# A pre-LN attention and GLU block: row-sum reciprocals and scalings two steps later, filler products ahead of a head group's first V products, and Q rows asked for at the third key tile

## Chip, cores and metric

One core of a Trainium2 chip. The metric is the device time of one execution in microseconds; the time of the kernel before is the median of three runs. The engines are PE (TensorE, matrix products), PEld (its weight loads), DVE (VectorE), ACT (ScalarE), POOL (GpSimd) and SP (SyncE, which here issues nearly all DMAs, in the program's order).

## The reference

A block of 2048 tokens and model width 512, with 32 heads of 16, followed by a gated layer of width 1792. All inputs are bfloat16.

```python
def _A_ref(x, wqkv, wo):
    B, S, D = x.shape
    H = 32
    Dh = D // H
    qkv = (lambda x, *d: x.transpose(*d))((x @ wqkv).reshape(B, S, 3, H, Dh), 2, 0, 3, 1, 4)
    q, k, v = qkv[0], qkv[1], qkv[2]
    scores = jnp.einsum("bhqd,bhkd->bhqk", q, k) * (Dh ** -0.5)
    p = _softmax(scores, axis=-1)
    o = jnp.einsum("bhqk,bhkd->bhqd", p, v)
    return (lambda x, *d: x.transpose(*d))(o, 0, 2, 1, 3).reshape(B, S, D) @ wo

def _B_ref(x, w_gate, w_up, w_down):
    g = jnp.einsum("bsd,df->bsf", x, w_gate)
    u = jnp.einsum("bsd,df->bsf", x, w_up)
    h = _sigmoid(g) * u
    return jnp.einsum("bsf,fd->bsd", h, w_down)

x = A_x
h = x + _A_ref(_layernorm(x, axis=-1), A_wqkv, A_wo)
h2 = h + _B_ref(_layernorm(h, axis=-1), B_w_gate, B_w_up, B_w_down)
return h2
```

With 32 heads and 2048 x 2048 scores each, the kernel takes 134 million exponentials, and these are what most of its time goes to.

## The kernel before

**Stages.** A prologue normalizes x and makes K of the first eight heads, the first Q rows and some of V. Then one long loop runs over the queries in five chunks (three of 512 columns, two of 256) and in each chunk over eight head groups of four heads. One unit is one key tile of one head: 128 keys against 512 queries, or two such tiles against 256 queries. Three units make a step; there are 683 steps (NS), and a head group takes 21.3 of them in a 512 chunk and 10.7 in a 256 chunk.

**A step** (the loop at L963). `emit_scores` (L764) issues the scores of three units into one of two PSUM buffers `pss` (L783) and one exponential of ACT over the whole buffer into a slot `pt` (L794). Every fourth step is split: two units go to ACT, and the third goes to DVE, which makes its exponential in parts: bits (L813) in the same step, the first part (L816, L819) one step later, the second (L822) two and the third (L826) three steps later. In the steps of the set `twice`, in all chunks but the first and at most every twelfth step, a second step of the cycle is split too, with scratch in `OT`.

**V products.** The tiles of probabilities are multiplied with V a cycle of four steps later, by a plan made at the start (`plan_pv`, L925). `emit_pv` (L857) adds 4 products for each key tile to the one accumulator `acc` (L864). Where the first key tile of a new group falls in the middle of a cycle, its V products are planned one step later than the rest (L933), since `acc` must be copied out first.

**The end of a head group.** After its last V products `emit_norm` (L834) copies `acc` to `xs_all` on DVE (L838), and SP sends the four row sums to DRAM (L841) and brings them back spread over 128 partitions (L842). Five steps later `recip` takes the reciprocals on DVE (L849), writes them to DRAM (L851) and reads them back broadcast, in four DMAs, to `rb_all` (L853). Five steps after that `scale` multiplies `xs_all` by `rb_all` into `OT` (L845), which the output projection reads (L506). `later(i, fn)` (L872) puts a function into the list `due` of step i.

**Q rows.** The scores read Q from two buffers `QB`, by turns. The rows of the next group are fetched by `emit_q_rows` (L217, four DMAs, L223) and `emit_q_bound` (L226, two DMAs, L233). In a 512 chunk these are issued in the program at key tile 12 of 16 of the running group (L788), in a 256 chunk at its first. SP does not wait for the step: it issues each DMA as soon as those ahead of it in its queue are out and what the DMA itself depends on is done.

**Filler.** What else there is to do (V, K and Q of the other heads, then for each finished chunk the output projection, the layer norm and the gated layer) is written as a generator, `filler` (L742), that yields costs and waits. `emit_fill` (L879) takes some of it in each step, by rates that depend on the step's place in its cycle of four and on how many V products the step has (L755). These products all use one PSUM bank, `pm`, so a new block waits until DVE or ACT has read the one before (up_mul L543, tanh L535, the copies L157, L430 and L551).

**Order within a step.** All engines run in the program's order (`manual_schedule`). In each step come first the scores and ACT's exponential, then the V products due, then the functions in `due`, then the filler (L969 to L974):

```python
for u in pv_due.pop(i, []):
    emit_pv(*u[:3], i)
for fn in due.pop(i, []):
    fn()
if 1 <= i < NS:
    emit_fill(i)
```

After the loop `ffn_last` (L652) does the last chunk's projection and gated layer by itself.

Of the kernel before, what the change touches and what calls it, by code (L numbers as in the profile page):

```python
# [18 lines left out]
def kernel(  # L19
# [19 lines left out]
    NG = H // 4  # L39
# [4 lines left out]
    NC = len(CHUNKS)  # L44
    NQC = S // QC
    GU = 3
    CYC = 4
    RATES = ((2.0, 2.0, 0.0, 3.0), (2.0, 2.5, 0.0, 3.0))
    FIRST = 44
    GM = 188  # L50
    G1 = 680
    QS = DH ** -0.5 * 1.4426950408889634 * 2.0 ** 23
    LEAD = 0.106445681
# [161 lines left out]
    qgs = [(c, g) for c in range(NC) for g in range(NG)]  # L215

    def emit_q_rows(n):  # L217
        c, g = qgs[n]
        q0, w = CHUNKS[c]
        assert ("q", q0 // QC, g // 2) in ready  # L220
        for j in range(4):
            r = 64 * (g % 2) + DH * j
            nc.sync.dma_start(out=QB[n % 2][32 * j:32 * j + 32:2, j, 0:w],  # L223
                              in_=QTu[r:r + DH, g // 2, q0:q0 + w])
# [167 lines left out]
    def per_bank(c):  # L392
        return QC // CHUNKS[c][1]
# [6 lines left out]
    NS = len(groups)  # L400
# [363 lines left out]
    def emit_scores(i):  # L764
        group = groups[i]
        n = len(group)
        pss = pss2[(i + 1) % 2]
        idle = i >= 3 * FIRST and (state["done"] or state["wait"] > i + CYC)
        pairs = i < FIRST or (i % 2 == 1 or i - i % CYC + 2 in twice) and not idle
        order = list(enumerate(group))  # L770
        if pairs and group[0][3] // 2 == group[1][3] // 2:
            order[1:] = order[:0:-1]
        n_of = max(per_bank(u[0]) for u in group)
        parts = [(ui, u, h) for h in range(n_of) for ui, u in order[:2] if h < per_bank(u[0])]
        parts += [(ui, u, h) for ui, u in order[2:] for h in range(per_bank(u[0]))]
        for ui, (c, g, k, j), h in parts:
            n_qg = c * NG + g
            w = CHUNKS[c][1]
            kt = k * per_bank(c) + h
            assert ("k", g // 2) in ready  # L780
            h0 = 64 * (j // 2)
            rows = slice(h0, h0 + 64) if pairs else slice(0, P)
            nc.tensor.matmul(pss[:, ui, h * w:(h + 1) * w], lhsT=KT[rows, g, kt * P:(kt + 1) * P],  # L783
                             rhs=QB[n_qg % 2][rows, j, 0:w], start=True, stop=True,
                             tile_position=(h0, 0) if pairs else None)
        for c, g, k, j in group:
            n_qg = c * NG + g
            if k == (12 if per_bank(c) == 1 else 0) and j == 3 and n_qg + 1 < len(qgs):  # L788
                emit_q_rows(n_qg + 1)
                emit_q_bound(n_qg + 1)  # L790
        slot = i % 7
        pt = pt4[slot] if slot < 4 else (pt_early if i < GM else pt_late)[slot - 4]
        na = n - 1 if i in split else n
        ex = nc.scalar.activation(out=pt[:, 0:na, :], in_=pss[:, 0:na, :], func=ACT.Exp, scale=DH ** -0.5 / QS)  # L794
        if na < n:
            scratch = scratch_of(i)
            tc.declare_no_dep(exp_bits(pss[:, na, :], *scratch).ins, ex.ins,
                              reason="both only read, from different banks")
            later(i + 1, lambda: exp_first(*scratch))
            later(i + 2, lambda: exp_second(*scratch))  # L800
            later(i + 3, lambda: exp_third(pt[:, na, :], *scratch))
        for ui, u in enumerate(group):
            p_of[u] = pt[:, ui, :]

    def scratch_of(i):
        if i % CYC:
            flat = OT[(int((i - 20) / SPC) + 1) % 2][:].rearrange("p g q -> p (g q)")
            return (flat[:, 0:2 * QC].bitcast(mybir.dt.int32), flat[:, 2 * QC:4 * QC].bitcast(mybir.dt.int32),
                    flat[:, 4 * QC:6 * QC].bitcast(FP32))
        return early_scratch if i < GM else late_scratch  # L810

# [17 lines left out]
    def norm_part(t, w, n):  # L829
        k = t.shape[1] * w // QC  # L830
        o = k * (n % (QC // w))
        return t[:, o:o + k]

    def emit_norm(c, g, i):  # L834
        w = CHUNKS[c][1]
        b = w // 32
        xs, rb, s32, r32 = (norm_part(t, w, g) for t in (xs_all, rb_all, s32_all, r32_all))
        nc.vector.tensor_copy(out=xs, in_=acc[:, 0:w])  # L838
        sd = dram.tile([4, w], FP32, name="sd", tag="sd%d" % w)
        for j in range(4):  # L840
            nc.sync.dma_start(out=sd[j:j + 1, :], in_=xs[32 * j + DH:32 * j + DH + 1, :])  # L841
        nc.sync.dma_start(out=s32, in_=sd[:].rearrange("j (a b) -> (j a) b", b=b))  # L842

        def scale():
            nc.vector.tensor_tensor(out=OT[c % 2][:, g, 0:w], in0=xs, in1=rb, op=ALU.mult)  # L845
            ready.add(("o", c, g))

        def recip():
            nc.vector.reciprocal(out=r32, in_=s32)  # L849
            rd = dram.tile([4, w], FP32, name="rd", tag="rd%d" % w)  # L850
            nc.sync.dma_start(out=rd[:].rearrange("j (a b) -> (j a) b", b=b), in_=r32)  # L851
            for j in range(4):
                nc.sync.dma_start(out=rb[32 * j:32 * j + 32, :], in_=rd[j:j + 1, :].to_broadcast([32, w]))  # L853
            later(i + 10, scale)
        later(i + 5, recip)

    def emit_pv(c, g, k, i):  # L857
        w = CHUNKS[c][1]
# [13 lines left out]
    def later(i, fn):  # L872
        due.setdefault(i, []).append(fn)
# [5 lines left out]
    def emit_fill(i):  # L879
        state["step"] = i  # L880
        r = rate(i)
        if not r or state["done"] or i < state["wait"]:
            state["debt"] = 0.0
            return
        state["debt"] += state["rate"] or r
        while state["debt"] > 0 or isinstance(state["next"], tuple):
            c = state["next"]
            state["next"] = next(fl, None)
            if c is None:
                state["done"] = True  # L890
                return
            if isinstance(c, tuple):
                kind, n = c
                if kind == "rate":
                    state["rate"] = n
                    continue
                state["debt"] = 0.0
                state["wait"] = i + 1 + n if kind == "gap" else i + 1 + (n - i - 1) % CYC if kind == "at" else n
                return
            state["debt"] -= c  # L900
# [5 lines left out]
    def load_w():  # L906
# [4 lines left out]
        for f in (0, 7):  # L911
            later(GM + 21 + f // 2, lambda f=f: nc.sync.dma_start(out=wd[:, f:f + 7, :], in_=wd_v[:, f:f + 7, :]))

    LAG = 2

    split = set(range(8, G1, CYC))
    twice = set()
# [7 lines left out]
    def plan_pv():  # L925
        plan, last = {}, 0
        for n, group in enumerate(groups):
            if n < G1:
                if n % CYC == 0:
# [12 lines left out]
    with tc.manual_schedule():  # L942
        p1ctx = ExitStack()
        pmh["pool"] = p1ctx.enter_context(tc.tile_pool(name="ps_p1", bufs=6, space=PSUM))
        prologue(p1ctx.enter_context(tc.tile_pool(name="pro", bufs=1)))
        p1ctx.close()
        pmh["pool"] = ps_misc
        sctx = ExitStack()
        ps_s = sctx.enter_context(tc.tile_pool(name="ps_s", bufs=1, space=PSUM))
        ptp = sctx.enter_context(tc.tile_pool(name="ptp", bufs=1))  # L950
        pss2 = [ps_s.tile([P, GU, QC], FP32, name=f"pss{k}") for k in range(2)]
        pt4 = [ptp.tile([P, GU, QC], BF16, name=f"pt{k}") for k in range(4)]
        for g4 in (0, 4):
            later(60 + g4, lambda g4=g4: nc.gpsimd.memset(wo_pad[:, g4:g4 + 4, :], 0.0))
        later(72, load_wo)
        for n in range(4):
            r = slice(32 * n, 32 * n + 32)
            nc.gpsimd.tensor_copy(out=same[r], in_=ident_bf[r, r].unsqueeze(1).to_broadcast([32, 4, H]))
        later(90, lambda: nc.gpsimd.tensor_copy(out=ident_f[:], in_=ident_bf[:]))
        load_w()  # L960
        pv_due = plan_pv()
        n_pv = {i: len(us) if i < G1 + CYC else 0 for i, us in pv_due.items()}
        for i in range(NS + LAG):  # L963
            if i < NS:
                emit_scores(i)
            if i == NS + LAG - 1:
                while next(fl) == 1:
                    pass
            for u in pv_due.pop(i, []):  # L969
                emit_pv(*u[:3], i)  # L970
            for fn in due.pop(i, []):
                fn()
            if 1 <= i < NS:
                emit_fill(i)  # L974
        for _ in fl:
            pass
        sctx.close()
        pmh["pool"] = ctx.enter_context(tc.tile_pool(name="ps_t", bufs=6, space=PSUM))
        pmh["work"] = ctx.enter_context(tc.tile_pool(name="tail", bufs=4))
        assert not due  # L980
        ffn_last(NC - 1)
# [30 lines left out]
```

## Time and profile before

| what | value |
|---|---|
| median of 3 runs | 963.77 us (963.26 to 965.14) |
| the profiled execution, its own time | 962.96 us |
| span of its instructions | 961.1 us |
| granted TensorE clock, mean | 1.000 |
| ACT busy, 35 to 100 us | 60.3 of 65.0 us |
| ACT busy, 932 us to the end | 5.8 of 29.1 us |
| first and last exponential of the loop start | 34.24 and 929.73 us |
| DMA, mean share of 16 engines over the span | q1 10.4%, q10 0.5% |

The span runs from the first instruction to the last; the time of the same execution is 1.86 us longer. In a row of a group of instructions stand line, engine and operation, the tiles it writes and reads with their shapes, the count, the busy time, the mean length in nanoseconds, and the engine's idle time just before these instructions with what ended it. In the timeline a row has start, length, engine, line and tiles, and in brackets the idle time ahead of it. Starts of PE's products of 512 columns lie about 0.215 us apart when nothing holds them up, although each row lasts some 0.38 us; the rows overlap.

### The profile page before, as it was taken

How to read it: one execution, taken by the hardware profiler on the slowest of the kernel's cores; microseconds unless marked ns; L12 is line 12 of the kernel's file. 1: busy time of each engine (PE TensorE's matmuls, PEld its weight loads, DVE VectorE, ACT ScalarE, POOL GpSimd, SP SyncE). 2: the span in 40 equal slices, each digit the busy share in tenths (PEclk: the TensorE clock that was granted, in tenths of full speed). 3: DMA queues.
4: the chain of work that ended last, by engine and by line, in shares of the span. 5: the costliest groups of instructions: out<-in, count | busy, mean ns of one | idle time of the engine just before them, and what ended most of it. 6: DMA issues, size and time to landing. Idle time of an engine off the chain costs nothing.

```text
span 961.1 us, 17150 instructions
## 1 busy us (share of the span) xinstructions
PE 826.7 (86%) x6327; PEld 337.8 (35%) x6425; DVE 788.1 (82%) x1428; ACT 895.3 (93%) x767; POOL 41.5 (4%) x49
## 2 busy tenths in 40 slices
PE   4887888888788999988788999988788999888998
PEld 2322222222222332222222233222355555455646
DVE  8589998888788888899888888888888788777653
ACT  4789999999999999999999999999998999899872
POOL 4700000000000000000000000000000000000000
PEclk9999999999999999999999999999999999999999
DMA  5001350000013000000011000001011000110010
GB/s 160 21 8 50 114 117 17 16 16 2 16 26 103 16 16 17 19 12 26 14 27 26 16 16 15 14 15 26 16 31 23 16 13 13 27 32 16 9 35 12
DMA packets 37500, 28.38 MB, mean 30 GB/s; under 512 B 17708, under 2 KB 32776, under 8 KB 37416
## 3 DMA queue, kind: packets, MB, share of 16 engines
q1 hardware_dynamic: 35828, 25.71, 10.4%
q10 hardware_dynamic: 1588, 1.58, 0.5%
q8 instruction: 50, 0.82, 0.4%
q14 instruction: 34, 0.28, 0.1%
HBM read 20.31 MB, written 2.61 MB: 24 GB/s over the span
## 4 chain that ended last, share of the span: by engine, by line
PE 40%; DVE 26%; ACT 23%; issue 7%; DMA 3%; SPq 1%; ACTq 0%; DVEq 0%; POOL 0%; POOLq 0%
PE pss L783 20%; ACT pt L794 12%; PE acc L864 8%; PE pm L530 6%; ACT stg L794 4%; ACT wd L794 4%; DVE stg L813 3%; ACT QTu L794 2%; PE pm L546 2%; DVE reg L816 2%; DVE st L139 2%; DVE pt L826 2%; DVE y L822 2%; PE pm L506 2%; DVE reg L543 1%
## 5 line engine op out<-in xcount | busy, mean ns | idle before, releaser
L783 PE MATMUL pss<-QB,KT 64*128 64x512 bf16 (+3 forms) x2542 | 475.8, 336 | 86.9 <-ACT pt L794 43.8
L794 ACT ACTIVATE pt<-pss 128x1536 bf16<-128x1536 f32 (+1 forms) x392 | 501.1, 1363 | 16.3 <-PE pss L783 12.0
L783 PEld LDWEIGHTS <-KT 64*128 64x128 bf16 (+1 forms) x2560 | 181.4, 95 | 345.3 <-issue 232.5
L794 ACT ACTIVATE stg<-pss 128x1536 bf16<-128x1536 f32 (+1 forms) x140 | 183.1, 1355 | 4.6 <-PE pss L783 3.8
L813 DVE TENSOR_SCALAR stg<-pss 128x512 int32<-128x512 f32 x123 | 84.8, 689 | 69.3 <-PE pss L783 53.0
L864 PE MATMUL acc<-pt,Vaug 128*17 128x512 bf16 (+1 forms) x1471 | 112.5, 338 | 4.5 <-DVE xs_all L838 3.2
L794 ACT ACTIVATE wd<-pss 128x1536 bf16<-128x1536 f32 (+1 forms) x80 | 103.8, 1390 | 2.7 <-PE pss L783 2.4
L794 ACT ACTIVATE QTu<-pss 128x1024 bf16<-128x1024 f32 (+1 forms) x71 | 95.5, 1345 | 1.7 <-PE pss L783 1.2
L819 DVE SCALAR_TENSOR_TENSOR y<-reg 128x512 f32<-128x512 f32 x123 | 85.2, 692 | 4.2
L822 DVE SCALAR_TENSOR_TENSOR y<-y,reg 128x512 f32<-128x512 f32 x123 | 84.2, 684 | 1.1
L864 PEld LDWEIGHTS <-Vaug 128*17 128x17 bf16 x2560 | 50.4, 89 | 96.1 <-issue 80.8
L530 PE MATMUL pm<-reg,reg 128*128 128x512 bf16 (+1 forms) x252 | 55.6, 333 | 8.7 <-DVE reg L543 6.6
L530 PE MATMUL pm<-reg,wu 128*128 128x512 bf16 (+1 forms) x280 | 58.1, 338 | 1.5 <-ACT sg L535 1.2
L546 PE MATMUL pm<-wd,reg 128*128 128x512 bf16 x173 | 51.2, 381 | 5.7 <-issue 2.9
L146 POOL TENSOR_TENSOR rs<-ve,pw_neg 128x1 f32<-128x1 f32 (+1 forms) x24 | 17.7, 736 | 888.9 <-DVE ve L144 758.0
L816 DVE TENSOR_SCALAR reg<-stg 128x512 int32<-128x512 int32 x123 | 52.0, 423 | 2.0
L864 PE MATMUL acc<-stg,Vaug 128*17 128x256 bf16 (+1 forms) x564 | 50.6, 326 | 0.6 <-DVE stg L826 0.4
L543 DVE SCALAR_TENSOR_TENSOR reg<-sg,pm 128x512 bf16<-128x512 f32 x56 | 38.2, 682 | 13.9 <-PE pm L530 13.5
L826 DVE SCALAR_TENSOR_TENSOR pt<-y,stg 128x512 bf16<-128x512 f32 x70 | 47.8, 683 | 1.8
L535 ACT ACTIVATE sg<-pm 128x512 f32<-128x512 f32 x56 | 35.6, 637 | 10.1 <-PE pm L530 9.8
L813 DVE TENSOR_SCALAR wd<-pss 128x512 int32<-128x512 f32 x45 | 30.9, 688 | 15.9 <-PE pss L783 14.9
L165 PE MATMUL pm<-reg 128*128 128x512 bf16 x112 | 35.6, 391 | 2.2 <-issue 0.8
(129 smaller groups left out, 707.5 us busy)
## 6 DMA issues: line engine op xcount, KB each, us to landing
rb_all<-rd SPq DMA_DIRECT2D x96, 64.0 KB
reg<-in_A_x_dram SPq DMA_DIRECT2D x8, 256.0 KB
xr<-in_A_x_dram SPq DMA_DIRECT2D x16, 128.0 KB
out_dram<-ob SPq DMA_DIRECT2D x15, 128.0 KB
rb_all<-rd SPq DMA_DIRECT2D x60, 32.0 KB
KT<-stg SPq DMA_DIRECT2D x7, 256.0 KB
reg<-in_B_w_gate_dram SPq DMA_DIRECT2D x4, 448.0 KB
wu<-in_B_w_up_dram SPq DMA_DIRECT2D x4, 448.0 KB
```

What stands on the lines that cost most here:

```text
L165: nc.tensor.matmul(ps[:], lhsT=wqkv_sb[:, c, w0:w0 + P], rhs=xnT[:, c, n * QC:(n + 1) * QC], start=(c == 0), stop=(c == DC - 1))
L530: nc.tensor.matmul(ps[:, i * w:(i + 1) * w], lhsT=wt[:, c, f * P:(f + 1) * P], rhs=hnT[:, c, 0:w], start=(c == 0), stop=(c == DC - 1))
L543: nc.vector.scalar_tensor_tensor(out=out, in0=a, scalar=1.0, in1=b, op0=ALU.add, op1=ALU.mult)
L546: nc.tensor.matmul(ps[:], lhsT=hT[:, f, tt * P:(tt + 1) * P], rhs=wd[:, f, :], start=(f == 0), stop=(f == FC - 1))
L783: nc.tensor.matmul(pss[:, ui, h * w:(h + 1) * w], lhsT=KT[rows, g, kt * P:(kt + 1) * P], rhs=QB[n_qg % 2][rows, j, 0:w], start=True, stop= ...
L794: ex = nc.scalar.activation(out=pt[:, 0:na, :], in_=pss[:, 0:na, :], func=ACT.Exp, scale=DH ** -0.5 / QS)
L813: return nc.vector.tensor_scalar(out=e_bits, in0=src, scalar1=ONE_BITS, scalar2=0.0, op0=ALU.add, op1=ALU.max)
L816: nc.vector.tensor_scalar(out=e_man, in0=e_bits, scalar1=0x7FFFFF, scalar2=-0x40800000, op0=ALU.bitwise_and, op1=ALU.bitwise_or)
L819: nc.vector.scalar_tensor_tensor(out=e_pol, in0=m, scalar=PA, in1=m, op0=ALU.add, op1=ALU.mult)
L822: nc.vector.scalar_tensor_tensor(out=e_pol, in0=e_pol, scalar=PB, in1=e_man.bitcast(FP32), op0=ALU.add, op1=ALU.mult)
L826: nc.vector.scalar_tensor_tensor(out=dst, in0=e_pol, scalar=PC, in1=e_bits.bitcast(FP32), op0=ALU.add, op1=ALU.mult)
L864: nc.tensor.matmul(acc[32 * j:32 * j + VW, 0:w], lhsT=Vaug[:, kt, 4 * g + j, :], rhs=p[:, h * w:(h + 1) * w], start=(kt == 0), stop=(kt == ...
```

## The change

Three edits.

1. `emit_norm` takes the reciprocals seven instead of five steps after the group's last V products, and the scaling twelve instead of ten. The last group of each chunk, and of the last chunk the last two, keep five and ten. That is 34 of the 39 groups that go through `emit_norm`.
2. In a step (from step 8 on) whose planned V products contain the first key tile of a group, the filler of this step is issued ahead of those V products, and not at the step's end. The rate is the same; where a step has three sets of V products it is 0, so nothing moves there. In the order in which the built program's instructions stand, 22 blocks of filler move: one to four products at 512 columns, or eight at 256.
3. In the chunks of 512 columns, Q rows for the next group are asked for at the third key tile (k == 2) of the running group from group 6 on (`EARLY`; groups are counted through all chunks). The 256 chunks keep the first key tile, the first six groups the thirteenth (k == 12).

```diff
+    EARLY = range(6, 64)
...
         for c, g, k, j in group:
             n_qg = c * NG + g
-            if k == (12 if per_bank(c) == 1 else 0) and j == 3 and n_qg + 1 < len(qgs):
+            if k == (0 if per_bank(c) > 1 else 2 if n_qg in EARLY else 12) and j == 3 and n_qg + 1 < len(qgs):
                 emit_q_rows(n_qg + 1)
                 emit_q_bound(n_qg + 1)
...
     def emit_norm(c, g, i):
         w = CHUNKS[c][1]
         b = w // 32
+        wait = 2 if g < NG - 1 - (c == NC - 1) else 0
...
-            later(i + 10, scale)
-        later(i + 5, recip)
+            later(i + 10 + wait, scale)
+        later(i + 5 + wait, recip)
...
-            for u in pv_due.pop(i, []):
+            us = pv_due.pop(i, [])
+            early_fill = i >= 2 * CYC and any(u[2] == 0 for u in us)
+            for u in us:
+                if early_fill and u[2] == 0:
+                    emit_fill(i)
                 emit_pv(*u[:3], i)
             for fn in due.pop(i, []):
                 fn()
-            if 1 <= i < NS:
+            if 1 <= i < NS and not early_fill:
                 emit_fill(i)
```

## The prediction

> **What bounds the kernel now.** First I read the page's busy shares and the stretches of the span.
>
> ```profile
> PE 826.7 (86%) x6327; PEld 337.8 (35%) x6425; DVE 788.1 (82%) x1428; ACT 895.3 (93%) x767; POOL 41.5 (4%) x49
> ...
> 100.00:600.00 500.00, 434.25 (x2762) 140.20 (x2811) 429.38 (x752) 496.32 (x420) 6.73 (x8) 1.00 0.12 31
> 600.00:700.00 100.00, 84.83 (x574) 29.14 (x581) 87.26 (x148) 97.18 (x82) 0.00 (x0) 1.00 0.07 17
> 700.00:932.00 232.00, 209.09 (x2340) 124.86 (x2368) 178.47 (x332) 218.00 (x186) 3.93 (x6) 1.00 0.09 22
> ```
>
> ACT, the exponentials, is the bound: between 100 and 600 us it is busy 496.3 of 500, and the clock column is 1.00 throughout. The change takes no work away, so it can only close idle time of ACT. That is the sum to look for, from the groups of ACT's instructions between 77 and 932 us (last numbers: idle before them, and what ended it).
>
> ```profile
> L794 ACT ACTIVATE pt<-pss 128x1536 bf16<-128x1536 f32 (+1 forms) x375 | 479.1, 1363 | 11.8 <-PE pss L783 7.6 <-issue 1.9 <-DVE y L819 0.6
> L794 ACT ACTIVATE stg<-pss 128x1536 bf16<-128x1536 f32 (+1 forms) x140 | 183.1, 1355 | 4.6 <-PE pss L783 3.8 <-ACT pt L794 0.2
> L794 ACT ACTIVATE QTu<-pss 128x1024 bf16<-128x1024 f32 (+1 forms) x71 | 95.5, 1345 | 1.7 <-PE pss L783 1.2
> ...
> L535 ACT ACTIVATE sg<-pm 128x512 f32<-128x512 f32 x49 | 31.5, 642 | 1.5 <-PE pm L530 1.2
> ```
>
> With 0.3 of a fifth group that is 19.9 us, mostly scores that came late. Everything below is a share of these 19.9. Third, the table of waits, for what the three edits aim at (total, times, longest):
>
> ```profile
> DVE r_all L849 <- DMA s_all<-sd: 6.6, 4, 2.5
> PE acc L864 <- DVE xs_all L838: 3.6, 8, 1.0
> DVE OT L845 <- DMA rb_all<-rd: 2.6, 1, 2.6
> PEld L783 <- DMA QB<-bnd: 1.5, 1, 1.5
> ```
>
> Last, each ACT gap over 0.1 us was followed back in the timeline. A step is one exponential of ACT (some 1.36 us), numbered as in the program.
>
> **Filler ahead of the first V products (22 steps).** At a new head group PE must wait until DVE has copied `acc`; filler stood behind the wait. Step 475:
>
> ```profile
> 644.32 0.68 DVE L838 COPY xs_all<-acc 128x512 f32<-128x512 f32 x1
> ...
> 645.06 0.61 PE L864 MATMUL acc<-pt,Vaug 128*17 128x512 bf16 x8 [0.95 <-DVE xs_all L838]
> ...
> 645.60 0.82 PE L546 MATMUL pm<-wd,reg 128*128 128x512 bf16 x3
> ...
> 646.26 0.81 PE L783 MATMUL pss<-QB,KT 128*128 128x512 bf16 x3
> ...
> 647.16 1.02 ACT L794 ACTIVATE pt<-pss 128x1024 bf16<-128x1024 f32 x1 [1.03 <-PE pss L783]
> ```
>
> PE could take new work at 643.94 (last score's start 643.73 plus a spacing of 0.21); the V products began at 645.06. The three filler products take 0.66 (645.60 to 646.26), less than that hole of 1.1. Run in it, they let the next scores start 0.66 earlier, and ACT's gap of 1.03 shrinks by 0.66. The same arithmetic (the smaller of hole and filler, and no more than the ACT gap that follows) at the other steps whose next exponential starts late:
> - step 539: hole 1.11, filler 0.87, but the filler's bank is only copied out at 727.37 (L157). Filler then runs to 728.30, V products (0.55) to 728.85, against 729.17: 0.32.
> - 367: 0.28 (all of that gap); 303: 0.18; 603: 0.13; 635: 0.09.
> - 27: filler 0.11, and the next filler, which waited for DVE's L451 after it, starts some 0.25 earlier; the gap is 0.68. I take 0.25.
>
> Sum 1.9 us. The other 15 steps are costed at nothing: ACT has no gap behind them, since an exponential of 1.36 us covers PE. What is late instead are V products, by the filler's time less the hole, at most 0.8 us; the next scores stand behind both either way. On DVE the order changes only three times for this edit, in the first chunk, where a filler's copies pass L826, whose result is read three steps later.
>
> **Scalings two steps later (34 of 39).** Where two exponentials of one cycle are split, DVE is full, and the scaling (L845, 0.68) fell between the parts:
>
> ```profile
> 627.02 0.68 DVE L845 TENSOR_TENSOR OT<-xs_all,rb_all 128x512 bf16<-128x512 f32 x1
> 627.62 0.68 DVE L822 SCALAR_TENSOR_TENSOR OT<-OT 128x512 f32<-128x512 f32 x1
> ...
> 628.34 0.69 DVE L826 SCALAR_TENSOR_TENSOR pt<-OT 128x512 bf16<-128x512 f32 x1
> ...
> 629.09 0.38 PE L864 MATMUL acc<-pt,Vaug 128*17 128x512 bf16 x1 [0.56 <-DVE pt L826]
> ...
> 630.10 1.45 ACT L794 ACTIVATE pt<-pss 128x1536 bf16<-128x1536 f32 x1 [0.57 <-DVE y L819]
> ```
>
> The V products of step 462 need L826's output; without L845 ahead it is there 0.6 earlier, PE's 0.56 and ACT's 0.57 go. In the changed order L845 stands behind that L826. Six such places, by their ACT gaps: 630.10 (0.57); 660.66 (0.23) and 413.98 (0.09), both with V products waiting for L826; and 330.83, 578.42, 789.66, where up_mul (L543) is late behind L845, so the gate products wait 0.7 for their bank, tanh starts 0.25, 0.25, 0.23 late and the next exponential another 0.11, 0.11, 0.12. Sum 1.96. Of the others the scaling lands in DVE's slack, or, at steps 314 and 506, at the start of such a cycle: bound from 0 to 0.68 each; I take 0, as those cycles do the same work before the next bits (L813) with or without the move.
>
> **Reciprocals two steps later (34).** DVE stands at the reciprocal until the row sums have come back, with all else queued behind it. One of the four waits reaches ACT: 0.76 before 833.21, then the 0.20 of the reciprocal itself, ahead of the copy at L551 that filler products waited 1.78 for, and ACT's gap before 836.06 is 1.95. Moved, 0.96 of it goes. The other three (1.39 before 535.21, 2.46 before 746.32, 2.00 before 877.71) have no ACT gap of their own behind them: 0. On the loss side, two steps later is the step with L816, L819 and up_mul; in the doubled cycles (norms of steps 238, 322, 430, 590) 0.2 more is put on a full DVE. Bounds 0 and 4 x 0.2 = 0.8; I take 0.8.
>
> **What else moves on SP.** The reciprocal issues one write and four reads of scratch (L851, L853), so these move too, and in the 256-column chunks the next group's Q rows now go before them. There SP is late today: at step 546 the row sums (L841) go out at 742.39, 3.6 us after their copy, behind rd, rb and Q rows. In the new order Q rows issue in SP's idle time and L841 about 1 us earlier. The scaling keeps its five steps behind the reciprocal, so its wait is as covered as before; the single wait of 2.6 is the last scaling, which does not move. One thing is worse: in group 2 the write goes behind a spread of K (0.5 MB). It would land some 2 to 3 us later, the Q rows behind it some 1 to 2; these were issued at 136.67 and are needed near 144.5. Cost 0, bound 1.
>
> **Q rows at the third key tile (groups 6 to 23).** Nothing waits for Q rows in the steady state: the one wait in the table lies at 33 us. Issue is now from about 12 us ahead of need. The earlier issue waits only for the scores of the group before, which are done by then, and takes some 3 us of SP while SP waits for DVE. 0 either way.
>
> **Sum.** 1.9 + 1.96 + 0.96 - 0.8 = 4.0 us. Span 961.1 - 4.0 = 957.1; this execution took 962.96 (1.86 around the span), so 958.9; the median shown, 963.77, lies 0.81 above it, so 959.8.
>
> **Rivals.**
> 1. The reciprocal's wait is an accident. From issue (L842) to the end of the wait it was 3.26 us at 829.95, but 1.68 at 744.64 and 1.64 at 876.07. At 1.7 the sums land at 831.65, before DVE is free at 832.45, and the 0.96 was nothing: 963.77 - 3.0 = 960.7. For it: two rows of four. 12%. The Trainium skill ("DMA: Bandwidth & Descriptors", "Anatomy of one DMA — SWDGE (gpsimd) path", a fit for DMAs that GpSimd issues) gives 2.0 us plus bytes for any DMA, by which the wait would not exist; this trace has 3.26 and 3.33 beside 1.64.
> 2. The gaps open again behind. PE is 90% busy after 700 us, and a closed gap leaves the next product on its own limit. At half retention 4.8 / 2 - 0.8 = 1.6: 962.2, no change that shows. Against it: at 475 and 462 the exponentials after the gap run back to back. 15%.
> 3. Slower: the moved scaling now stands right ahead of the second part (L822) of the running split in nearly all 34 groups. If that makes L826 late for its V products, each costs 0.56 (the row at 629.09). It decides from (4.8 + 1.9) / 0.56 = 12 of 34; at 15 it is 963.77 + 8.4 - 4.8 = 967.4. For it: DVE is 86% busy from 100 to 600. Against: L826 comes in its split's fourth step and its V products at least three steps, 4 us, later. 8%.
> 4. The K spread in group 2, with DVE or PE waiting 2 us on what it delays, 961.8: 5%.
>
> **How the numbers follow.** The forecast has 60%. 959.8 is its number; its own range is 958 to 961.5 (bounds of the scaling, reciprocal and SP terms). A measurement of this kernel tells 0.2%, 1.9 us, from no change. Faster by more: the forecast, rival 1 and a little: 73%. Within: rivals 2 and 4, 19%. Slower: rival 3, 8%. The range 957.6 to 963.6 reaches over rivals 1, 2 and 4 and leaves out rival 3 and a gain beyond all terms.
>
> **What would show it.** PE's wait for xs_all falls from 3.6 to under 1 us and ACT's gap at step 476 from 1.03 to about 0.4. No gap over 0.2 at step 463; tanh waits (1.5) halve. DVE waits for s_all vanish, the gap at step 617 falls to 1.0. ACT's idle time between 77 us and its last exponential falls from 19.9 to near 16. Wrong would be: PE waits for L826 of pt, stg and QTu that grow past their 2 us, scores that wait for QB, or ACT idle unchanged with the old waits gone.

## The result, and the profile after

The change made the kernel slower, not faster.

| | before | after |
|---|---|---|
| median of 5 runs each | 963.77 us (963.26 to 966.53) | 971.67 us (970.26 to 975.46) |
| ratio, 95% interval | | 1.0081 (1.0055 to 1.0106) |
| the profiled execution | 962.96 us, span 961.1 | 972.09 us, span 970.3 |
| start of the last exponential | 929.73 us | 936.31 us |
| from there to the end of the span | 31.3 us | 34.0 us |

Of the 9.2 us by which the spans differ, 6.6 were lost before the last exponential starts and 2.6 behind it. The stretches of the span after the change, with the same columns as before (busy time of PE, PEld, DVE, ACT and POOL, then the granted clock):

```profile
100.00:600.00 500.00, 432.39 (x2732) 137.29 (x2779) 425.89 (x742) 490.65 (x414) 6.96 (x8) 0.99 0.12 30
600.00:700.00 100.00, 86.45 (x557) 28.06 (x566) 88.67 (x150) 98.05 (x83) 0.00 (x0) 1.00 0.07 20
700.00:932.00 232.00, 209.60 (x2319) 123.88 (x2348) 181.44 (x334) 217.33 (x186) 4.03 (x6) 0.99 0.09 20
```

Between 600 and 700 us ACT is busier than before (98.05 against 97.18): there the change gains. From 100 to 600 it gets six instructions less done (414 against 420), and two stretches have a clock of 0.99 that was 1.00. So the loss comes in places. The groups of ACT's instructions in the loop name the tiles that they fall on:

```profile
L795 ACT ACTIVATE pt<-pss 128x1536 bf16<-128x1536 f32 (+1 forms) x375 | 479.6, 1368 | 10.0 <-PE pss L784 6.8 <-issue 1.2
L795 ACT ACTIVATE stg<-pss 128x1536 bf16<-128x1536 f32 (+1 forms) x140 | 183.7, 1363 | 7.0 <-PE pss L784 6.3
L795 ACT ACTIVATE QTu<-pss 128x1024 bf16<-128x1024 f32 (+1 forms) x71 | 96.0, 1352 | 5.1 <-PE pss L784 4.9
L795 ACT ACTIVATE wd<-pss 128x1024 bf16<-128x1024 f32 (+1 forms) x68 | 88.1, 1389 | 3.7 <-PE pss L784 3.4
```

The pt group idles less than before (10.0 against 11.8). But stg went from 4.6 to 7.0, QTu from 1.7 to 5.1, and wd from 0.3 to 3.7. ACT still waits for scores; the question is what held the scores up. The table of waits (total, times, longest) says it:

```profile
DVE OT L847 <- DMA rb_all<-rd: 9.9, 4, 5.3
...
DVE reg L516 <- DMA xr<-in_A_x_dram: 4.0, 2, 2.4
...
DVE r_all L851 <- DMA s_all<-sd: 1.2, 1, 1.2
...
PE acc L866 <- DVE xs_all L840: 1.1, 3, 0.5
```

The last two are the waits that the change aimed at, and they fell, from 6.6 and 3.6. The first was one wait of 2.6 and is now four of 9.9. The second, DVE waiting for the rows of x that the residual needs (`xr`, L516), is new. These six waits (four and two) are for transfers that SP issues in order: `rb`, the reads of the reciprocal that follow its write `rd`, and the loads of `xr` close behind them. All but one of 0.24 belong to four stalls.

**Group 2, at 141 us.** SP's queue before, and then after:

```profile
128.51 0.32 SPq L851 DMA_DIRECT2D rd<-r_all  x1
129.95 1.71 SPq L853 DMA_DIRECT2D rb_all<-rd  x4
131.71 1.84 SPq L904 DMA_DIRECT2D wo_pad<-in_A_wo_dram  x4
133.65 1.19 SPq L206 DMA_DIRECT2D KT<-stg  x2
```

```profile
126.46 1.79 SPq L906 DMA_DIRECT2D wo_pad<-in_A_wo_dram  x4
131.02 1.20 SPq L207 DMA_DIRECT2D KT<-stg  x2
132.32 0.56 SPq L853 DMA_DIRECT2D rd<-r_all  x1
137.29 1.72 SPq L855 DMA_DIRECT2D rb_all<-rd  x4
```

DVE, PE and ACT after (start, length, what it waited for in brackets):

```profile
140.91 0.69 DVE L847 TENSOR_TENSOR OT<-xs_all,rb_all 128x512 bf16<-128x512 f32 x1 [3.10 <-DMA rb_all<-rd]
...
143.82 0.85 PE L784 MATMUL pss<-QB,KT 128*128 128x512 bf16 x3 [3.18 <-DVE wd L814]
...
144.76 1.45 ACT L795 ACTIVATE wd<-pss 128x1536 bf16<-128x1536 f32 x1 [2.30 <-PE pss L784]
```

The write stands behind four loads of wo and the K spread. SP can issue the reads only when the write has landed, 4.97 us after its issue; before, the two were 1.44 apart, ahead of wo and K. The scaling (L847) waits 3.10, and with it all that DVE has queued behind, down to the bits (L814) of the next split exponential, which free the bank that PE's next scores need.

**Groups 16 and 24, at 521 and 731 us.** Here it is the load behind `rb` that is late. Before:

```profile
509.27 0.34 SPq L851 DMA_DIRECT2D rd<-r_all  x1
510.73 1.71 SPq L853 DMA_DIRECT2D rb_all<-rd  x4
512.49 1.45 SPq L511 DMA_DIRECT2D xr<-in_A_x_dram  x1
...
517.02 0.68 DVE L515 TENSOR_TENSOR reg<-pm,xr 128x512 f32<-128x512 f32 x1
```

After:

```profile
513.88 0.34 SPq L853 DMA_DIRECT2D rd<-r_all  x1
...
516.71 1.92 SPq L855 DMA_DIRECT2D rb_all<-rd  x4
...
518.69 0.88 SPq L512 DMA_DIRECT2D xr<-in_A_x_dram  x2
521.05 0.69 DVE L516 TENSOR_TENSOR reg<-pm,xr 128x512 f32<-128x512 f32 x1 [1.59 <-DMA xr<-in_A_x_dram]
...
525.43 0.40 PE L157 MATMUL pm<-ident_bf,xn 128*128 128x128 bf16 x4 [1.91 <-DVE xn L151]
...
526.95 1.45 ACT L795 ACTIVATE stg<-pss 128x1536 bf16<-128x1536 f32 x1 [1.83 <-PE pss L784]
```

Before, this load went out at 512.49 and DVE took it up at 517.02, 4.5 us later. Now it goes out at 518.69, and DVE, done at 519.45, needs it 0.8 us later. Group 24 is the same (issue 729.01; before 720.06 for a use at 724.16): DVE waits 2.43 and ACT 2.91.

**The tail.** The write of group 37 now follows an out store, and the queue falls behind by one more group:

```profile
923.89 0.36 SPq L554 DMA_DIRECT2D out_dram<-ob  x1
...
924.35 0.37 SPq L853 DMA_DIRECT2D rd<-r_all  x1
...
927.85 1.71 SPq L855 DMA_DIRECT2D rb_all<-rd  x4
...
929.61 1.16 SPq L843 DMA_DIRECT2D sd<-xs_all  x4
...
940.19 0.42 DVE L847 TENSOR_TENSOR OT<-xs_all,rb_all 128x256 bf16<-128x256 f32 x1 [5.28 <-DMA rb_all<-rd]
```

3.50 us from write to reads (1.42 before). Group 38's sums, copied out of `acc` by 926.63 (L840, 926.20 and 0.43 long), leave only at 929.61, and its scaling, the last before the tail, ends DVE's wait of 5.28 (2.57 before). ACT's idle time at L680 goes from 2.1 to 4.9.

ACT's gaps at the first three stalls are 2.30 + 0.90, 1.83 + 0.89 + 0.67 and 2.91: 9.5 us. The tail adds 2.7. Up to the last exponential ACT idled 26.3 us, 7.0 more than before (19.3 by the same count); so 9.5 - 7.0 = 2.5 us of gaps did close.

### The profile page after: what moved, and what is told of

It is laid out like the page before. It is cut to its first block, busy times and chain, and to the rows that moved or that the text cites. A ratio compares the mean times of both kernels' runs of the same rounds, so it can differ in the third digit from the quotient of the medians.

```text
span 970.3 us, 17170 instructions
## 1 busy us (share of the span) xinstructions
PE 832.7 (86%) x6326; PEld 336.0 (35%) x6425; DVE 791.6 (82%) x1428; ACT 895.1 (92%) x767; POOL 41.9 (4%) x49
## 4 chain that ended last, share of the span: by engine, by line
PE 41%; DVE 24%; ACT 23%; issue 7%; DMA 4%; SPq 1%; ACTq 0%; DVEq 0%; POOL 0%; POOLq 0%
PE pss L784 20%; ACT pt L795 12%; PE acc L866 8%; PE pm L531 6%; ACT stg L795 4%; ACT wd L795 4%; DVE stg L814 2%; DMA rd<-r_all 2%; PE pm L547 2%; DVE y L823 2%; ACT QTu L795 2%; DVE st L140 2%; PE pm L507 1%; DVE pt L827 1%; DVE reg L817 1%
## 5 line engine op out<-in xcount | busy, mean ns | idle before, releaser
L814 DVE TENSOR_SCALAR stg<-pss 128x512 int32<-128x512 f32 x123 | 84.8, 689 | 68.4 <-PE pss L784 59.5
L817 DVE TENSOR_SCALAR reg<-stg 128x512 int32<-128x512 int32 x123 | 51.4, 418 | 2.1
L814 DVE TENSOR_SCALAR wd<-pss 128x512 int32<-128x512 f32 x45 | 31.0, 688 | 15.7 <-PE pss L784 14.2
```

The lines of the kernel that those rows point to most:

```text
L814: return nc.vector.tensor_scalar(out=e_bits, in0=src, scalar1=ONE_BITS, scalar2=0.0, op0=ALU.add, op1=ALU.max)
L817: nc.vector.tensor_scalar(out=e_man, in0=e_bits, scalar1=0x7FFFFF, scalar2=-0x40800000, op0=ALU.bitwise_and, op1=ALU.bitwise_or)
```

## The experiments

The theory: edits 2 and 3 are harmless and the scalings gain; the loss comes from the reciprocal's write and reads, moved to a worse place in SP's queue. Its rivals: the early Q rows reorder SP; the fillers or the moved scaling hold DVE or PE; the loads are slow in themselves. All ratios are against the kernel before, run beside each; the kernel before had medians of 964.0 to 964.4 us there.

| run | what | median, us | ratio (95%) |
|---|---|---|---|
| e1_no_norm | edits 2 and 3 | 962.83 | 0.9979 (0.9969 to 0.9988) |
| e2_norm_only | edit 1 | 970.76 | 1.0077 (1.0058 to 1.0096) |
| e3_scale_only | all, reciprocal at 5 steps | 960.26 | 0.9964 (0.9952 to 0.9975) |
| e4_xr_pool | all, xr loads on POOL | 964.87 | 1.0008 (0.9995 to 1.0022) |
| e5_group2 | e4, group 2 at 5 steps | 963.82 | 0.9996 (0.9984 to 1.0008) |
| e6_tail | e5, group 37 at 5 steps | 961.04 | 0.9970 (0.9959 to 0.9981) |
| e7_rd_pool | all, rd and rb on POOL | 987.12 | 1.0241 (1.0225 to 1.0257) |
| e8_no_q | e3 without edit 3 | 961.63 | 0.9973 (0.9961 to 0.9984) |
| e9_scale_again | e3 again | 960.79 | 0.9964 (0.9951 to 0.9978) |
| e10_three_late | e3, three groups at 7 steps | 960.23 | 0.9961 (0.9947 to 0.9975) |
| e11_q_alone | edit 3 | 963.78 | 1.0000 (0.9990 to 1.0011) |
| e12_fill_alone | edit 2 | 962.24 | 0.9985 (0.9973 to 0.9997) |

**Which edit loses.** Four kernels, from the changed one and from the one before:

```diff
 e1_no_norm (from after)
-        wait = 2 if g < NG - 1 - (c == NC - 1) else 0
+        wait = 0
 e2_norm_only (from before)
+        wait = 2 if g < NG - 1 - (c == NC - 1) else 0
-            later(i + 10, scale)
-        later(i + 5, recip)
+            later(i + 10 + wait, scale)
+        later(i + 5 + wait, recip)
 e3_scale_only (from after)
-        later(i + 5 + wait, recip)
+        later(i + 5, recip)
 e4_xr_pool (from after)
-        nc.sync.dma_start(out=xr[:], in_=x_v[:, t, :])
+        nc.gpsimd.dma_start(out=xr[:], in_=x_v[:, t, :])
```

> The changed kernel with reciprocal and scaling put back to five and ten steps after the norm; fillers first and early Q rows stay. Theory: the loss of 7.9 us comes from the later reciprocal, whose write and reads of scratch (L853, L855) stand in SP's queue behind the K spread and out stores and ahead of the xr loads; without it the four stalls (before the exponentials at 144.8, 527.0 and 733.8 us, and the tail) are gone and the filler's 1.9 us remains: 962 (961 to 963). Rival Q: the early Q rows (L224) reorder SP and cause the stalls: about 970, xr loads late again. Rival F: the fillers ahead of the V products cause them: about 970.

> The kernel before with the later reciprocals and scalings alone. Theory: the stalls all come, the filler's gain is missing and the scaling's stays: 971.7 + 1.9 = 973.5 (970 to 975). Rivals Q and F: without early Q rows and fillers no stall: about 960.8 (963.8 less 3.0).

> The changed kernel with the reciprocal back at five steps and the scaling left at twelve, so that it comes seven steps after the reciprocal. Theory: the scaling costs nothing by its place; its gain of 2.0 us comes on top of the filler's 1.9: 960 (959 to 961.5), and DVE's waits for rb_all are at most the last one of 2.6. Rival S: the moved scaling, ahead of L822's part of the split, is what loses: 966 to 972.

> The changed kernel with the xr loads (L512) issued from POOL instead of SP. Theory: DVE's waits for xr (1.6 and 2.4) and with them the ACT gaps of 3.4 at 527 to 532 us and 2.9 at 733.8 us go; the stall at 144.8 us and the tail stay: 971.7 - 6.3 = 965.4 (964.5 to 967). If the loads are slow in themselves, or DVE and PE are late there for another reason: no change, 971.7.

Without edit 1 the change gains 2.0 us (0.9979); edit 1 alone brings nearly the whole loss (1.0077), less than the 973.5 foretold but inside its range. The fillers and the Q rows are cleared, and so is the scaling: kept at twelve steps with the reciprocal back at five, the kernel is faster than before by 0.36%. Its waits, to be set beside those of the changed kernel:

```profile
DVE r_all L851 <- DMA s_all<-sd: 5.2, 4, 2.6
DVE OT L847 <- DMA rb_all<-rd: 2.7, 1, 2.7
```

The old waits for the row sums are back, and they cost little (more on step 617 below); the waits for `rb_all` are down to the last group's, and there is none for `xr`. The two kernels differ in the reciprocals alone: 1.0081 / 0.9964 = 1.0117, some 11.3 us for moving them by two steps.

With `xr` on a queue of its own (e4_xr_pool) no wait for it is left, ACT's gaps at 527 and 734 us are gone, and the ratio falls from 1.0081 to 1.0008, 7.0 us against the 6.3 of those gaps. The reciprocals are as late there as in the changed kernel. So two of the four stalls are a matter of who stands behind whom on SP.

**The other two stalls.** On top of e4_xr_pool the reciprocals of single groups go back:

```diff
 e5_group2 (e6_tail: in (2, 37))
-        later(i + 5 + wait, recip)
+        later(i + (5 if c * NG + g == 2 else 5 + wait), recip)
```

> The changed kernel with the xr loads on POOL (as in e4_xr_pool) and the reciprocal of group 2 alone back at five steps, so that its write to scratch stands ahead of wo_pad and the K spread again. Theory: the stall of DVE at the scaling of group 2 (3.1 us at 140.9) goes, and with it ACT gaps of 1.4 (in e4_xr_pool) to 3.2 (in the changed kernel): 964.9 - 1.4 to 3.2 = 962.6 (961.7 to 963.5). If the K spread does not delay it: 964.9 and DVE still waits for rb_all by 140 us.

> e5_group2 and the reciprocal of the last group but one (37) back at five steps, ahead of the out store again. Theory: the tail's ACT gap at L680 falls from 5.3 to 2.1 and the time by 3.2 more: 959.4 (958.5 to 960.5). All other reciprocals still come two steps later; if they have a price of their own, such as 0.8 for the doubled cycles, it stays above e3_scale_only's 960.3; if their own gain of 0.7 at step 617 counts, it is below. If the tail is late for another reason: 962.6, gap of 5.3 unchanged.

Group 2 was worth 1.1 us by the medians (964.87 to 963.82), less than foretold; by the ratios' intervals it can't be told from nothing. The mechanism itself shows in the trace of e5_group2: the write (129.85) and the reads (131.29) are 1.44 apart again, and the scaling waits for nothing (0.03). The price had been read from one execution; in e4_xr_pool the write's landing was 4.34, the scaling's wait 2.26 and ACT's gap 1.43, in e2_norm_only 3.84, 1.77 and 0.95, both without a second gap. The tail was worth 2.8 (963.82 to 961.04): the write of group 37 at 911.22, its reads at 912.70, ACT's idle time at L680 back to 2.15. In e6_tail 32 of the 34 reciprocals are still two steps later, and it stands 0.6 us (0.9970 against 0.9964) behind e3_scale_only, with intervals that overlap. Late reciprocals cost nothing that shows once no queue is disturbed.

**Taking the reciprocal off SP's queue.**

```diff
-            nc.sync.dma_start(out=rd[:].rearrange("j (a b) -> (j a) b", b=b), in_=r32)
+            nc.gpsimd.dma_start(out=rd[:].rearrange("j (a b) -> (j a) b", b=b), in_=r32)
-                nc.sync.dma_start(out=rb[32 * j:32 * j + 32, :], in_=rd[j:j + 1, :].to_broadcast([32, w]))
+                nc.gpsimd.dma_start(out=rb[32 * j:32 * j + 32, :], in_=rd[j:j + 1, :].to_broadcast([32, w]))
```

> The changed kernel with the write and the reads of the reciprocal (L853, L855) issued from POOL, so that SP never waits for the reciprocal. Theory: the loss is from places in SP's queue, not from the later reciprocal; the waits for xr go, and the write no longer stands behind the K spread and the out stores: 959.5 to 961.5, as e3_scale_only. Rival: it is the traffic itself (transfers at the same time) or the lateness of the reciprocal: then the stalls by 141 us and in the tail (together 4.6 to 6) stay, 965 or more; should POOL's issues land later than SP's, DVE waits for rb_all in many groups and it is slower than 971.

A miss, by its last branch: 987.12. The waits for `xr` did go, but POOL is a slower issuer. It waits 2.0 us a group for the write to land (76.9 over 39 groups; on SP, before, 45.6) and each of four reads takes 0.51; DVE waited for `rb_all` 14 times, 27.5 us together, among them the scaling of group 8, with an ACT gap of 3.48 behind it. The stalls of group 2 and of the tail (there DVE waits 6.08 before 953.15) stayed, as the rival in the expectation had it. Group 2:

```profile
140.54 1.18 SPq L207 DMA_DIRECT2D KT<-stg  x2
141.43 0.57 POOL L853 DMA_DIRECT2D rd<-r_all  x1 [21.12 <-DVE reg L817]
147.13 1.97 POOL L855 DMA_DIRECT2D rb_all<-rd  x4 [5.12 <-DMA rd<-r_all]
151.22 0.69 DVE L847 TENSOR_TENSOR OT<-xs_all,rb_all 128x512 bf16<-128x512 f32 x1 [3.89 <-DMA rb_all<-rd]
155.68 1.45 ACT L795 ACTIVATE wd<-pss 128x1536 bf16<-128x1536 f32 x1 [3.70 <-PE pss L784]
```

The write goes out from POOL, 0.9 us behind SP's K spread, and the reads follow only 5.70 us later; from 140 to 147 us the DMA share is 1.08, so the 16 DMA engines are full. In group 37 the two are 3.41 apart (937.70 and 941.11), with SP's out store at 937.33. So in these two groups another issuing queue does not help; what both kernels share there is the transfers issued just ahead of the write.

The largest gap, 7.06 before 125.69, is of another kind (timeline of POOL and DVE):

```profile
113.25 1.82 POOL L956 MEMSET wo_pad<- 128x2048 bf16 x1
113.34 7.25 DVE L817 TENSOR_SCALAR reg<-wd 128x512 int32<-128x512 int32 x1
```

POOL's four clears of `wo_pad` and `KT` (1.82 us each, to 120.31) had come late behind group 1's reads, and DVE's L817, 0.42 us elsewhere, took until the last of them was over.

**What the Q rows and the fillers do.**

```diff
 e8_no_q (from e3_scale_only)
-            if k == (0 if per_bank(c) > 1 else 2 if n_qg in EARLY else 12) and j == 3 and n_qg + 1 < len(qgs):
+            if k == (0 if per_bank(c) > 1 else 12) and j == 3 and n_qg + 1 < len(qgs):
 e10_three_late (from e3_scale_only)
-        later(i + 5, recip)
+        later(i + (7 if c * NG + g in (26, 32, 35) else 5), recip)
 e11_q_alone (from before)
-            if k == (12 if per_bank(c) == 1 else 0) and j == 3 and n_qg + 1 < len(qgs):
+            if k == (0 if per_bank(c) > 1 else 2 if n_qg in range(6, 64) else 12) and j == 3 and n_qg + 1 < len(qgs):
 e12_fill_alone (from after, with the condition on k of e8_no_q)
-        wait = 2 if g < NG - 1 - (c == NC - 1) else 0
+        wait = 0
```

e9_scale_again is e3_scale_only unchanged.

> e3_scale_only with the Q rows back at the thirteenth key tile: fillers first and scalings two steps later alone. Theory: the place of the Q rows is worth nothing: 960.3 (959.5 to 961.2). If the early Q rows help or harm, it differs from e3_scale_only by more than 1.

> e3_scale_only once more, beside the three that follow: 960.3 (959.5 to 961.5). It gives the spread between chips and sessions of the same kernel.

> e3_scale_only with the reciprocals of groups 26, 32 and 35 alone two steps later, the three of the last chunks whose row sums DVE waited for (2.46, 0.76 and 2.00 in the kernel before) and whose writes do not pass an xr load. Theory: the gain foretold for the reciprocal is real where no queue is disturbed; the ACT gap at step 617 falls from 1.85 to 1.15: 959.6 (958.8 to 960.5), 0.7 below e9_scale_again. If late reciprocals cost anything on DVE: above it.

> The kernel before with the early Q rows alone. Theory: no change that can be measured, 963 to 965, ratio 0.999 to 1.001. Rival: the 1.4 between e3_scale_only and e8_no_q is theirs: 962.5 or less, ratio 0.9985 or less.

> The kernel before with the fillers ahead of a new head group's V products alone. Theory: 1.9 us less than before: 962.2 (961.5 to 963.2), ACT gap before step 476 0.7 and before step 540 about 1.0. If the gaps open again behind: 963 to 964.

The Q rows alone change nothing (1.0000, 0.9990 to 1.0011). The 1.4 us between e8_no_q and e3_scale_only was spread: e9_scale_again, the same kernel as the latter, came to 960.79, and the intervals overlap. The fillers alone gain 1.4 us (0.9985): ACT's gap before step 476 is 0.38, before step 540 1.09. In e10_three_late the gap at step 617 is 1.15, 0.70 less than in e3_scale_only as expected, and DVE's waits for the row sums are down to one of 0.2; 0.56 us beside e9_scale_again is in the right direction and less than can be told apart. But the gap to compare with depends on the execution: with that reciprocal at five steps it is 1.85 in e3_scale_only, 1.26 in e9_scale_again, the same kernel, where DVE did not wait for these sums, and 1.42 to 1.95 in the others; with seven steps it is 1.15 in every trace. From step 649 to step 657 it is alike: 13.6 to 14.2 us with the reciprocals at five steps (13.89 in e9_scale_again), 13.5 in every trace with seven. At 960.2 us it and e3_scale_only are the fastest of these kernels, 0.4% under the kernel before.

## Why the prediction was wrong

**Fillers: right.** 1.9 foretold, 1.4 measured alone (0.3 to 2.6 by the interval) and 2.0 with the Q rows. By single gaps: step 476 1.03 to 0.38 for a foretold cut of 0.66, step 540 1.32 to 1.09 for 0.32, step 368 0.28 to 0.11 for 0.28. Three small ones did not close: steps 304, 604 and 636 (0.18, 0.13 and 0.09 foretold) went from 0.31 to 0.33, stayed at 0.13, and went from 0.24 to 0.35. In the changed kernel step 476 stands at 0.71, and so it does in e3_scale_only: the moved scalings take 0.3 of it back, which no term held.

**Scalings: right.** 1.96 foretold; between e1_no_norm and e3_scale_only the ratio falls by 0.0015, 1.4 us, with intervals that overlap. The gap at step 463 (0.57) and the waits of the three late tanh (0.25, 0.25, 0.23) are gone in the changed kernel, and in e1_no_norm, without the move, they are there. Rival 3, the moved scaling ahead of the split's second part, did not come.

**Reciprocals on DVE: right in kind, the size an accident.** The gap at step 617 fell to 1.15, as "falls to 1.0" had it. But 0.96 was one execution's price: beside the traces with five steps (1.26 to 1.95) the move is worth 0.1 to 0.8 there, as rival 1 held, at 12%. The 0.1 to 0.7 between steps 649 and 657, just behind a wait that was priced at nothing (2.00 before 877.71), was not foreseen. The 0.8 put against it for the doubled cycles shows in no run.

**What else moves on SP: here the prediction failed.** Its sentence was "Cost 0, bound 1", and moving the reciprocals cost some 11.3 us (the changed kernel against e3_scale_only). Three steps of that paragraph went wrong:

- "The scaling keeps its five steps behind the reciprocal, so its wait is as covered as before." Five steps, 6.8 us, cover a write that lands in 1.4 us and the reads behind it. They did not cover the writes of groups 2 and 37, which landed in 4.97 and 3.50, now behind other transfers; in group 7, with nothing large just ahead, a landing of 3.38 left no wait. The order was known for group 2, and the delay was put at "some 2 to 3 us"; it was 3.5 more (4.97 against 1.44), on top of an issue two steps later, and it was charged to the Q rows behind it and not to the scaling that needs it. Rival 4 had this mechanism, with a price of 2 us for one place and 5%; the price in the profile was 3.2.
- The out stores (L553) were not looked at. Two steps later the write of group 37 is behind one: 2.8 us by e6_tail.
- The `xr` loads (L511) were not looked at either, and they are the largest part, 7.0 us by e4_xr_pool. Moving a pair of DMAs with a wait for landing between them back by two steps also moves back all that stands behind the pair. The row was in the trace of before: `rb` at 510.73, `xr` at 512.49, used at 517.02. Its slack was 4.5 us less a landing of about 2.4 (518.69 to 521.05 when DVE waited for it): some 2.2 us, less than two steps of 1.36.

These three account for it: 7.0 (e4), 1.2 (e5) and 2.5 (e6), each by the ratios, make 10.7 of the 11.3 us between the changed kernel and e3_scale_only; the 1.2 is within its noise. Without the reciprocals the prediction's sum would have given 963.77 - 1.9 - 1.96 = 959.9; that kernel has 960.3.

**The rest.** Q rows at 0: right. "DVE waits for s_all vanish": one of 1.2 is left. The sign by which the prediction said it would fail, "ACT idle unchanged with the old waits gone", is close to what came: the old waits went, and ACT idled more.

What stays open: from issue of the write to issue of the reads it took 2.8 to 3.4 us in group 16 in every kernel with its reciprocal at seven steps on SP, and 1.4 to 1.5 in every one with five, though no large transfer stands just ahead of it on SP there, in e4_xr_pool not even the load of `xr`. Of DVE's wait of 1.59 for `xr` there, 1.4 hang on that. Group 24 is alike (2.36 against 1.40). The kernel before has such landings too, of 2.3 to 3.1 in groups 6, 7 and 14, with no wait of the scaling behind them. No run tells why.

## What to carry to other kernels

When an instruction that issues DMAs is moved, write out the order of its queue before and after for every place it happens, not for one: what it now stands behind, and what stands behind it with how much slack between issue and use. A write that is read back through memory holds an in-order queue until it has landed, so it is a wait on that queue, and everything behind inherits its delay. It landed late behind large transfers whichever engine issued it (4.97 us on SP, 5.70 on POOL): another queue frees what stands behind the write, as it did for `xr`, and not the write. Waits of an engine that end in slack (6.6 us of DVE here, worth 0.1 to 0.8 at the one gap that was priced) are a poor reason to move anything that other queues lean on.

## What the hardware showed

A stall can cost more than its length, because the granted clock may fall behind it. The stretches around group 2 in the changed kernel:

```profile
140.00:143.80 3.80, 0.61 (x3) 0.11 (x2) 2.72 (x5) 2.35 (x2) 0.00 (x0) 1.00 0.82 267
143.80:146.00 2.20, 2.18 (x17) 0.49 (x18) 2.10 (x5) 1.24 (x1) 0.00 (x0) 0.66 0.01 2
146.00:148.00 2.00, 2.00 (x10) 0.54 (x7) 1.70 (x3) 1.10 (x2) 0.00 (x0) 0.53 0.00 0
```

PE is idle from 140.6 to 143.8, and the clock is 1.00 while it waits. For the next 4 us, with PE full, it is 0.66 and then 0.53. Three score products that took 0.60 at 137.50 take 1.04 at 145.99, and ACT has a second gap of 0.90 behind the first of 2.30. The same comes after PE's 1.91 at 525.4 (0.76, then 0.50) and its 2.56 at 731.9 (0.60, then 0.75), both followed by PE that is late again.

But a pause is neither enough nor needed. In the same trace PE waits 2.40 before 940.67, and the clock stays at 1.00; so it does behind 2.34 before 144.39 in e4_xr_pool, group 2 again. And in e1_no_norm it falls where PE's longest pause was 0.59:

```profile
487.10:490.50 3.40, 2.13 (x13) 0.70 (x10) 3.18 (x5) 3.40 (x4) 0.00 (x0) 1.00 0.36 98
490.50:493.90 3.40, 3.24 (x18) 0.64 (x17) 2.60 (x5) 2.90 (x3) 0.00 (x0) 0.53 0.00 0
```

An ACT gap of 0.80 follows at 494.43. No run tells what decides it. Such drops also part the executions of one kernel: of the 25 of the kernel before beside e9_scale_again to e12_fill_alone, the 11 with a mean clock of 1.000 took 961.8 to 963.3 us, the 11 with 0.998 963.8 to 964.7, and the 3 below that 965.4 to 967.4.

The Trainium skill ("TensorE: Matmul & The Clock Gate", "Part 1: The HAM clock gate") has the clock at one half after an idle window of some 3.4 us. The half agrees with the 0.50 to 0.53 here; the pauses ahead of the drops (1.91 to 3.18, and 0.59 at most in e1_no_norm) are shorter than that page's window.

POOL can stop DVE outright. In the changed kernel the same L817 takes 2.28 us at 46.60, beside a clear of `wo_pad` from 45.05 and one of `KT` from 46.80, and in e7_rd_pool the 7.25 shown above; every other one of that line, in both, is at most 0.50. Other DVE work ran beside POOL (L814 at 44.79, in 0.68, beside a clear). The Trainium skill ("SBUF — State Buffer", "SBUF: two separate sides") has a pair of ports that DVE's fast modes and POOL take in turns, for a whole instruction, the loser blocked; the two rows agree, but for one thing: DVE was held over four instructions of POOL on end.
